# Sigmoid attention and a routed MoE on one core: the splitting block's arm of the run-time loop laid first, the full block's third

## The chip, the cores and the metric

The kernel runs on one core of a Trainium2 chip. The metric is the device time of one execution in microseconds; of several runs the median is given. The profile is of one execution.

## The reference

The first part is attention with a sigmoid in place of the softmax, for 8 batches of 12 heads with 448 tokens of 64 numbers. The second is a mixture of experts over the 3584 resulting tokens of 768 numbers: a token whose skip score is positive goes to the one expert, of eight, with the largest logit.

```python
scores = scale * np.matmul(q, k.transpose(0, 1, 3, 2)) - np.log(S)
attn = 1.0 / (1.0 + np.exp(-scores))
x = np.matmul(attn, v)                      # then as (B * S, H * D)

do_compute = (x @ w_skip) > 0
xc = x[do_compute]
e_idx = np.argmax(xc @ w_gate, axis=1)
for e in range(E):
    h = np.maximum(xc[e_idx == e] @ w1[e], 0.0)
    y[e_idx == e] = gate_w * (h @ w2[e])    # gate_w: softmax weight of the chosen expert
out[do_compute] = xc + y
```

## The kernel before

**Attention.** 48 steps, one for each batch and pair of heads, compute scores (L217), the sigmoid on ACT (L237) and the product with the values (L245). Behind each batch come its logits and its routing: each chosen token's number and gate weight are written to a list in DRAM that has a row range for each expert.

**Experts in straight code.** The expert with the most tokens by an early count is the first one; its weights are loaded and split during attention into a high and a low part (`wh1`, `wl1`, `wh2`, `wl2`). Two blocks of 128 of its tokens are done in straight code behind attention (`b_ph`, `b_py` in the profile). Meanwhile VectorE works out a plan for the rest (L847 to L1050): which block comes in which iteration of a loop, and of which kind it is. The table `slots` gets for each iteration its kind and the next expert to load.

**The loop.** L1493 runs over the remaining blocks. In each iteration every engine reads the kind from `slots` into a register (`entry`, L1054, called in L1494) and branches by itself: first at L1482 on `kind < HALF`, then at L1483 or at L1488. There are four kinds:

- FULL: a block of up to 128 tokens of the expert whose split weights are in place (`block(i, False)`), with three matmuls for each pair of tiles (high by high, low by high, high by low);
- SPLIT: the same, but it is the last full block of its expert, so while it goes on, ACT and VectorE split the next expert's raw weights over the old ones (`block(i, True)`, L1194 to L1203);
- HALF and FEW: up to 64 or up to 32 tokens of an expert that are left over, with unsplit weights (L1414 and L1347). These arms also issue the next expert's weight loads on SP's queue (L1176, L1185).

FULL and SPLIT issue the same matmuls on TensorE: 36 at L496, 48 at L523, 14 transposes, in a slightly different order (`lag` in `gemm1`).

**How the arms lie.** Each engine has an instruction stream of its own. In it the loop is laid out so: the head (hint for the branch at the back edge, reading of the kind, branch of L1482), the branch of L1483, the first arm of the first inner If; then the branch of L1488, and both arms of the second inner If; then the second arm of the first inner If; then the tail, which counts the iteration and branches back at L1493. Before, that is FULL, HALF, SPLIT, FEW. The arms but the last end in a jump to the tail; the profile shows it under the line of the inner If. An arm's first instruction follows the untaken branch where the inner If holds, and is reached by a taken one where it doesn't.

**The order around it.** The order inside an arm is written out by hand (`manual_schedule`, L1477). Between iterations there is no barrier: engines run on by semaphores. `f_last` (L1002) is the kind written for a whole block: a positive value, when the next block is the start of another expert, becomes SPLIT, anything else stays 0, which is FULL. The kinds of the other blocks come from L910 (`HALF - FEW` times a flag, plus `FEW`).

## Time and profile before

| | us |
|---|---|
| median of 3 runs | 535.46 |
| the three runs | 531.62, 535.46, 537.47 |
| the profiled execution | 538.86 |
| its span, from first to last instruction | 537.2 |
| TensorE (PE) busy in it | 506.3 |
| VectorE (DVE), ScalarE (ACT), GpSimd (POOL) busy | 296.9, 274.0, 259.5 |
| mean granted TensorE clock | 0.981 |

A row of the profile names an engine and a line of the kernel. PEld is TensorE's weight load, which runs beside the matmuls (PE). A name with a q (PEldq, ACTq) is the engine's sequencer, that is, the branches, waits and register operations in its queue; those aren't counted as busy. In the chain of waits, each entry is what released the next one; "issue" is time in which the engine waited for nothing that the profile shows. Attention and the straight code take the span up to about 325 us, the loop the rest.

### The profile page before, as it was taken

The numbers are of one execution on the slowest core, as the hardware profiler recorded it, in microseconds if no ns is written. First come the engines' busy times: TensorE is split into PE (matmuls) and PEld (weight loads), VectorE is DVE, ScalarE is ACT, GpSimd is POOL, SyncE is SP. The second block draws the span as 40 slices with busy tenths as digits, with TensorE's granted clock in tenths as the row PEclk, the third lists the DMA queues.
The fourth block names the chain that finished last, engine by engine and source line by source line (L and its number), as shares of the span: only waits on it lengthen the run. The fifth ranks groups of instructions, "written<-read, shape, count | busy, mean of one in ns | idle before, by whom it ended". The sixth has DMA issues, their size and how long they took to land.

```text
span 537.2 us, 15241 instructions
## 1 busy us (share of the span) xinstructions
PE 506.3 (94%) x4985; PEld 337.0 (63%) x4986; DVE 296.9 (55%) x732; ACT 274.0 (51%) x483; POOL 259.5 (48%) x413
## 2 busy tenths in 40 slices
PE   7999999999999999999999998999999999999970
PEld 5555555555555555556446986859587878787850
DVE  4555758568586795675856922962213232369321
ACT  3676766767767566666662122922212323177220
POOL 3523554345566874666674140453324444455642
PEclk8999999999999999999999998999999999999995
DMA  7999897798999899998964046688493959595930
GB/s 207 202 232 221 174 200 152 153 185 176 206 207 233 191 212 197 192 224 168 216 111 95 1 128 245 227 246 299 128 380 108 378 165 381 175 393 163 366 75 7
DMA packets 140481, 107.67 MB, mean 200 GB/s; under 512 B 97013, under 2 KB 112795, under 8 KB 140432
## 3 DMA queue, kind: packets, MB, share of 16 engines
q1 hardware_dynamic: 134096, 97.88, 70.0%
q0 software_dynamic: 4576, 8.66, 7.1%
q8 instruction: 31, 0.51, 0.4%
q10 hardware_dynamic: 1760, 0.48, 0.4%
q14 instruction: 18, 0.15, 0.1%
HBM read 98.93 MB, written 17.60 MB: 217 GB/s over the span
## 4 chain that ended last, share of the span: by engine, by line
PE 74%; DMA 9%; DVE 4%; SPq 4%; issue 3%; ACT 2%; POOL 1%; ACTq 0%; POOLq 0%; DVEq 0%
PE s L217 16%; PE pa L245 14%; PE ph L496 12%; PE py L523 11%; DMA out_dram<-y 4%; PE b_ph L496 3%; PE b_py L523 3%; PE py L1347 3%; PE ph L1347 3%; SPq L268 2%; PE pxt L472 2%; PE py L1414 2%; PE ph L1414 2%; DVE x L202 1%; DMA wr<-in_moe_w_dram 1%
## 5 line engine op out<-in xcount | busy, mean ns | idle before, releaser
L237 ACT ACTIVATE at<-s,bias 128x896 f32<-128x896 f32 x192 | 172.0, 914 | 84.6 <-PE s L217 82.3
L217 PE MATMUL s<-x 64*64 64x448 f32 (+1 forms) x1536 | 166.1, 501 | 7.0 <-DVE x L202 3.3
L245 PE MATMUL pa<-at,v 64*64 64x448 f32 (+1 forms) x1536 | 162.2, 490 | 0.0
L184 POOL COPY kq<-kq 32x896 f32<-32x896 f32 (+1 forms) x96 | 88.2, 919 | 104.6 <-DMA kq<-in_q_dram 62.0
L217 PEld LDWEIGHTS s<-x 64*64 64x64 f32 x1536 | 79.0, 191 | 63.7 <-issue 26.4
L245 PEld LDWEIGHTS pa<-at,v 64*64 64x64 f32 x1536 | 62.0, 133 | 55.7 <-issue 47.6
L202 DVE STREAM_TRANSPOSE x<-kq 128x448 f32<-128x448 f32 x94 | 83.0, 945 | 13.7 <-POOL kq L184 11.8
L255 DVE TENSOR_TENSOR xt<-xt,pa 128x448 f32<-128x448 f32 x48 | 29.5, 614 | 46.1 <-ACT xt L642 42.3
L394 POOL DMA_INDIRECT lst<-rec,idx x32 | 32.3, 1009 | 18.3 <-issue 10.5
L466 POOL TENSOR_TENSOR wl<-wr,wh 128x384 fp32r<-128x384 f32 (+1 forms) x28 | 31.7, 1143 | 8.9 <-DVE wh L465 7.7
L260 DVE STREAM_TRANSPOSE y<-xt 128x448 f32<-128x448 f32 x48 | 31.0, 646 | 4.4 <-DMA out_dram<-y 2.6
L550 POOL DMA_INDIRECT out_dram<-ys,rp x15 | 23.7, 1578 | 15.8 <-issue 8.2
L505 ACT ACTIVATE hs<-ph 128x512 f32<-128x512 f32 x14 | 8.4, 598 | 43.9 <-PE ph L496 35.9
L523 PE MATMUL py<-wh,hh 128*128 128x384 f32 x112 | 29.8, 346 | 0.0
L516 DVE TENSOR_TENSOR hl<-pht,hh 128x512 fp32r<-128x512 f32 x14 | 9.7, 690 | 36.0 <-ACT hh L515 27.6
L523 PE MATMUL py<-wh,hl 128*128 128x384 f32 x112 | 28.8, 338 | 0.0
L523 PE MATMUL py<-wl,hh 128*128 128x384 f32 x112 | 28.7, 337 | 0.0
L496 PE MATMUL ph<-wh,xh 128*128 128x512 f32 x84 | 26.3, 410 | 2.6 <-issue 2.6
L496 PE MATMUL ph<-wl,xh 128*128 128x512 f32 x84 | 27.2, 410 | 0.0
L482 DVE TENSOR_TENSOR xl<-pxt,xh 128x384 fp32r<-128x384 f32 x30 | 15.3, 552 | 20.7 <-PE py L1347 8.9
L642 ACT ACTIVATE xt<-pa 128x448 f32<-128x448 f32 x48 | 25.7, 536 | 1.9 <-PE pa L245 1.3
L496 PE MATMUL ph<-wh,xl 128*128 128x512 f32 x84 | 25.2, 404 | 0.0
(273 smaller groups left out, 666.9 us busy)
## 6 DMA issues: line engine op xcount, KB each, us to landing
raw<-in_moe_w_dram SPq DMA_DIRECT2D x64, 768.0 KB
v<-in_v_dram SPq DMA_DIRECT2D x48, 256.0 KB
out_dram<-y SPq DMA_DIRECT2D x192, 56.0 KB
kq<-in_k_dram SPq DMA_DIRECT2D x46, 224.0 KB
kq<-in_q_dram SPq DMA_DIRECT2D x46, 224.0 KB
wr<-in_moe_w_dram SPq DMA_DIRECT2D x12, 256.0 KB
wr<-in_moe_w_dram SPq DMA_DIRECT2D x16, 192.0 KB
lst<-fill SPq DMA_DIRECT2D x4, 464.0 KB
```

The source lines that it names most:

```text
L184: nc.gpsimd.tensor_copy(a[BT:, :, :, :BT], a[:BT, :, :, BT:])
L202: nc.vector.transpose(xs[:, n].rearrange("p (r j) -> p j r", j=NJ), t.rearrange("p (j d) -> p j d", d=D)[:, :, :BT],)
L217: nc.tensor.matmul(sc[m * D : (m + 1) * D, j, : qs.stop - qs.start], xs[r, 0, first::NR7], xs[r, 1, qs], start=True, stop=True,)
L237: nc.scalar.activation(at[:, :, :n], sc[:, :, :n], AF.Sigmoid, bias=bias, scale=SCALE)
L245: nc.tensor.matmul(pa[j * D : (j + 1) * D, r, qs], vt[rs, j, r + c if c < 3 else 3 * (1 - r), :], at[rs, j, : qs.stop - qs.start], start=( ...
L255: nc.vector.tensor_tensor(x, x, pa[:, 1, :S], op=ALU.add)
L260: nc.vector.transpose(y, xts[b][:, hp, :])
L394: put = nc.gpsimd.indirect_dma_start(out=lst[:, :], out_offset=bass.IndirectOffsetOnAxis(ap=idx[:, c : c + 1], axis=0), in_=rec[:, c, :], ...
L466: nc.gpsimd.tensor_tensor(lo, r, hi, op=ALU.subtract)
L496: nc.tensor.matmul(ph[h], a[:, j * P : (j + 1) * P], w[j][h], start=(n == 0), stop=(n == len(t) - 1),)
L523: last = nc.tensor.matmul(py[:, o, :H2], a[h][:, js], w[j][:, o * H2 : (o + 1) * H2], start=(j == 0 and n == 0), stop=(j == NK2 - 1 and n ...
L1347: nc.tensor.matmul(dst[g * SM : (g + 1) * SM, :n], a, w, start=(j == 0), stop=(j == most - 1), tile_position=(0, g * SM),)
```

## The change

The kinds are renumbered so that SPLIT is 0 and FULL is 3; FEW and HALF keep 1 and 2. The arms of SPLIT and FULL change places in `choose`, so that the streams hold SPLIT, HALF, FULL, FEW. `f_last` is computed with the opposite comparison: a positive value becomes 0 (SPLIT), anything else becomes 3 (FULL). The bound given for the kind, the largest number, is 3 as it was. What the arms compute, and in which order the blocks come, is the same.

```diff
-    FULL, FEW, HALF, SPLIT = range(4)
+    SPLIT, FEW, HALF, FULL = range(4)
...
-    V.tensor_scalar(f_last, f_last, 0.0, float(SPLIT), op0=ALU.is_gt, op1=ALU.mult)
+    V.tensor_scalar(f_last, f_last, 0.0, float(FULL), op0=ALU.is_le, op1=ALU.mult)
...
     arms = {
+        SPLIT: lambda i: block(i, True),
         FULL: lambda i: block(i, False),
-        SPLIT: lambda i: block(i, True),
         HALF: half,
         FEW: few,
     }
...
         with tc.If(kind < HALF) as c:
             with tc.If(kind < FEW) as d:
-                run(FULL, i)
+                run(SPLIT, i)
             with d.Else():
                 run(FEW, i)
         with c.Else():
-            with tc.If(kind < SPLIT) as d:
+            with tc.If(kind < FULL) as d:
                 run(HALF, i)
             with d.Else():
-                run(SPLIT, i)
+                run(FULL, i)
...
-        kind = entry(TYP, ds(i + 2, 1), mybir.ALL_ENGINES, SPLIT)
+        kind = entry(TYP, ds(i + 2, 1), mybir.ALL_ENGINES, FULL)
```

## Prediction

> **What bounds the kernel now.** I read the page first, for the engine that has no slack, then the chain of waits around the start of the loop, then the branches of the lines that the change touches.

> ```profile
> span 537.2 us, 15241 instructions
> PE 506.3 (94%) x4985; PEld 337.0 (63%) x4986; DVE 296.9 (55%) x732; ACT 274.0 (51%) x483; POOL 259.5 (48%) x413
> ...
> q8 instruction: 31, 0.51, 0.4%
> ```

> PE works for 94% of the span. q8 is a queue that carries code: 31 pieces, 0.51 MB, so 16 KB each. The chain from 322 us on (start, length, what):

> ```profile
> 322.07 3.16 PE b_py L523 x18
> 325.23 2.54 issue
> 327.77 8.08 PE ph L496 x27
> ...
> 340.53 7.37 PE py L523 x42
> 347.90 5.30 PE ph L1414 x24
> ...
> 360.13 6.50 PE ph L496 x27
> ...
> 466.62 2.91 PE py L1347 x32
> 469.53 6.50 PE ph L496 x27
> ```

> Almost everything in it is PE. The one hole in the loop is at its entry: 2.54 us in which PE waits for nothing that the profile knows. Inside the loop one iteration follows the other without a gap: 340.53 + 7.37 is 347.90, where the next arm's matmuls (L1414, `half`) begin, and 466.62 + 2.91 is 469.53. So what is saved or lost on PE in the loop moves the end by as much.

> The lines of the choice show what the hole is. First the branch at L1488 at the entry, then at the end of the first iteration, then later; last L1482 over the whole loop (count, min/median/max in ns, first and last start):

> ```profile
> L1488 ACTq COMPARE_BRANCH  x1: 93/93/93, 323.7 to 323.7; - x1
> L1488 PEldq COMPARE_BRANCH  x1: 3435/3435/3435, 324.2 to 324.2; - x1
> L1488 DVEq COMPARE_BRANCH  x1: 122/122/122, 327.3 to 327.3; - x1
> ...
> L1488 PEldq COMPARE_BRANCH  x2: 73/136/198, 344.6 to 346.3; - x2
> ...
> L1488 PEldq COMPARE_BRANCH  x5: 73/193/209, 356.7 to 484.8; - x5
> ...
> L1482 PEldq COMPARE_BRANCH  x14: 74/83/397, 323.7 to 511.8; - x14
> ```

> The first iteration goes past L1482 to L1488 and from there to the arm of kind 3: a splitting block. On PE's queue that jump took 3.435 us; later ones on this line took 0.073 to 0.209 us. On ACT and DVE the same jump took 0.093 and 0.122 us. So it is PE's own code. The code queue, over the stretches 0 to 324, 322 to 326 and 332 to 334 us:

> ```profile
> q8 instruction: 29, 0.48, 0.7%
> ...
> q8 instruction: 1, 0.02, 2.0%
> ...
> q8 instruction: 1, 0.02, 2.9%
> ```

> With PE's counts up to the loop, and in one FULL, one HALF and one FEW arm (us, busy and count of PE, PEld, DVE, ACT, POOL, then PE's clock, DMA share, GB/s):

> ```profile
> 0.00:322.70 322.70, 313.45 (x3714) 185.99 (x3716) 212.74 (x510) 198.79 (x267) 169.44 (x210) 0.99 0.84 178
> ...
> 417.30:435.50 18.20, 18.20 (x98) 16.26 (x97) 4.54 (x14) 5.00 (x14) 6.91 (x20) 1.00 0.86 325
> 348.00:360.10 12.10, 11.98 (x67) 5.25 (x65) 7.64 (x17) 4.87 (x16) 6.61 (x13) 1.00 0.69 192
> 409.50:417.00 7.50, 6.82 (x88) 4.11 (x85) 3.16 (x12) 2.46 (x12) 4.55 (x11) 1.00 0.61 159
> ```

> 3714 + 3716 instructions over 29 pieces is 256 a piece: while PE works through one piece, about one is fetched. A block arm is 195 matmuls and weight loads, HALF 132, FEW 173, and each has some 20 to 35 waits and register operations besides (an estimate from the counts of such rows). I take 215, 165 and 210: the loop is 820 instructions with its head and tail, 3.2 pieces. FULL and HALF together are 380, so the splitting arm begins 1.5 pieces behind the loop's head. That was too far: one piece came at 322 to 326 us while the branch waited, the last one between 332 and 334, and between 340 and 537 us the code queue has no row at all. From there on the whole loop stays where PE can reach it.

> **The change part by part.** The sums are made against the profiled execution: 538.86 us, a span of 537.2 and 1.66 around it. The median shown is 535.46, 3.4 less, and the three runs lie between 531.62 and 537.47; a difference of these sums is carried over to the median as it is.

> *The entry.* The splitting arm is now the first: L1482 and L1483 aren't taken (74 to 83 ns at L1482), and PE runs on into the arm. It is there at 324.0, and the matmuls ahead last until 325.23. The operands are ready too:

> ```profile
> 323.03 1.02 DVE L482 TENSOR_TENSOR xl<-pxt,xh 128x384 fp32r<-128x384 f32 x2 [3.41 <-ACT xf L1062]
> ```

> So the 2.54 us go.

> *The clock behind the hole.*

> ```profile
> 322.50:325.90 3.40, 2.71 (x16) 2.39 (x14) 1.67 (x4) 0.85 (x7) 0.00 (x0) 1.00 0.02 5
> 325.90:329.30 3.40, 1.53 (x7) 1.29 (x8) 0.49 (x1) 0.00 (x0) 1.04 (x1) 1.00 0.78 237
> 329.30:332.70 3.40, 3.40 (x10) 2.62 (x9) 0.00 (x0) 0.00 (x0) 0.00 (x0) 0.50 1.04 371
> ```

> In 325.9 to 329.3 PE was busy for 1.53 of 3.40 us, and for the next 3.4 us it was granted half its clock. The first 27 matmuls took 8.08 us where the same group takes 6.50 at 360.13: 1.58 us, and these go with the hole. Gain so far: 2.54 + 1.58 = 4.12 us.

> *The arm's far end.* Every arm ends in a jump to the loop's tail. Before, the tail lay one FEW arm (210, 0.8 piece) behind the splitting arm; now HALF, FULL and FEW lie between, 590 instructions or 2.3 pieces. [...] I expect the wait of the entry to come again here: 3.435 in place of the 0.198 of the row from 344.6, so 3.24 more. What covers it: that jump starts at 344.6, PE's queued work lasts until 347.90, and the next arm's first wait starts at 346.6:

> ```profile
> L1414 PEldq EVENT_SEMAPHORE  x6: 51/51/51, 346.6 to 347.8; - x6
> ```

> So 1.3 us at most are spare, less some of these waits; I take 1.1, and PE stands idle for 2.1 us (1.9 to 2.4). Half the clock can follow, for 0 to 1.58 us: the busy share ahead of the throttled stretch was 45%, ahead of an unthrottled one 80%, and a hole of 2.1 us leaves between 38% and 70% of a 3.4 us stretch busy, by where it falls. Net: -4.12 + 2.1 + (0 to 1.58) = -2.0 to -0.4. I take the middle, -1.2.

> [...]

> *The FULL arms.*

> ```profile
> L1483 PEldq COMPARE_BRANCH  x15: 73/189/224, 358.3 to 511.9; - x15
> ```

> Of the 14 iterations, the 8 branches at L1488 (one into and one out of an arm) make 4, two of them splitting; the 15 at L1483 (two of a FULL arm, one of a FEW arm, behind which the tail follows at once) make five FULL and five FEW. The FULL arms now pass two taken branches (about 0.2 us each) where they had two untaken ones (0.08), some 0.25 us more each, and the second splitting arm 0.25 less. PE's queue hides that: at 469.53 the old splitting arm, which took both, followed a FEW arm, the shortest cover, without a gap. If it weren't hidden it would be 5 x 0.25 - 0.25 = 1.0 us. On ACT, DVE and POOL the arms trade places in loops whose branches never waited (93 and 122 ns above). SP leaves the first iteration with nothing to issue until 350.78, so a wait of a few us there is covered.

> ```profile
> 350.78 0.39 SPq L1176 DMA_DIRECT2D raw<-in_moe_w_dram  x1
> ```

> *The kinds.* L1002 keeps one instruction with another comparison and constant; the table has the same size. Nothing.

> **The rivals.** *The tail is there in time* (-4.1 us: 531.3). For it: the arm runs for 20 us, and PE keeps more than two pieces. Against it: up to 324 us the pieces came one for one with the work, and 1.5 pieces ahead of it nothing was there.

> *The new fetch stands behind the expert's weights* (slower). The entry's fetch met an idle DMA (share 0.02). The new one falls at 344.6 - 4.1 = 340.5, when the weights still arrive:

> ```profile
> 340.20:343.60 3.40, 3.40 (x23) 3.40 (x21) 3.40 (x7) 3.36 (x8) 2.60 (x5) 1.00 0.63 243
> 343.60:347.00 3.40, 3.40 (x21) 3.40 (x20) 3.05 (x6) 3.40 (x7) 2.52 (x4) 1.00 0.43 120
> ```

> For it: behind the entry's jump (over at 327.6) the next piece came only after 332, 4.4 us on, with the DMA at 0.78 to 1.04. Against it: by 343.6 most of the weights are in. If the fetch waits for that, the stall grows by up to 343.6 - 340.5 = 3.1 us: -4.12 + 2.1 + 3.1 + 1.58 = +2.7, 538.1. With half the clock behind the hole, it is slower than before from 0.4 us of waiting on.

> *It isn't the code's distance*: the first branch of a loop is slow wherever it goes (L1482 too had its 397 ns at the entry). Then the wait stays at the entry and nothing changes, 535.5. Against it: the piece fetched in just that stretch, and the other engines' quick jumps.

> **How the numbers follow.** Wait moved to the arm's end, -2.0 to -0.4: 0.5, 534.3. Gain kept, -4.1: 0.2, 531.3. Behind the weights, up to +2.7: 0.2, 538.1. Nothing: 0.1, 535.5. The range, 530.7 to 538.7, takes in all four with 0.6 us on either side for the spread of the runs. A change of 1% is 5.4 us, about what a measurement of this kernel can tell from none; no case reaches it, and only the spread of runs could carry the second (faster 0.07) or the third (slower 0.05) beyond it; same 0.88.

> **What would show it.** Right: no "issue" row of over 0.3 us at the loop's entry, full clock there, no L1488 or L1483 branch of PE over 0.5 us near 324, but one of 3 us or more at the first arm's end, with an "issue" row of about 2 us ahead of L1414 and a code piece in the same stretch. Wrong: a long branch still at 324; or none anywhere (then 531); or one of over 4 us (then above 535.5). If the entry's hole goes and the end doesn't move although no new hole is seen, PE wasn't the bound there, and my first step fails.

## The result, and the profile after

The changed kernel is a little slower: a median of 537.65 us over 14 runs (534.08 to 541.18) against 533.56 over 14 runs of the kernel before (531.22 to 537.47). The ratio is 1.0069, with a 95% interval from 1.0046 to 1.0092, or +3.7 us (+2.5 to +4.9). Its profiled execution took 536.12 us, 534.4 of them span.

The wait moved as forecast, and it is larger in its new place. PE's branch into the first splitting block, now on L1483, and its jump at that block's end (count, min/median/max in ns, first and last start):

```profile
L1483 PEldq COMPARE_BRANCH  x1: 68/68/68, 321.9 to 321.9; - x1
...
L1483 PEldq COMPARE_BRANCH  x1: 5247/5247/5247, 338.4 to 338.4; - x1
```

The 3435 ns of the entry have become 68; the 198 ns of the jump at the end have become 5247. Two windows from the entry on (us, busy and count of PE, PEld, DVE, ACT, POOL, then PE's clock, DMA share, GB/s) show PE without a gap and at full clock:

```profile
322.90:326.30 3.40, 3.40 (x16) 2.59 (x15) 1.14 (x2) 0.00 (x0) 1.04 (x1) 1.00 0.56 142
326.30:329.70 3.40, 3.40 (x18) 2.71 (x17) 0.00 (x0) 1.05 (x2) 0.00 (x0) 1.00 0.98 330
```

The HALF arm that follows, in order of time on PE (start, length, what, in brackets the idle time before it):

```profile
345.70 8.36 PE L1414 MATMUL ph<-raw,xf 128*64 128x512 f32 x24 [4.02 <-issue]
```

The same 24 matmuls took 5.30 us before. Why they take longer stands in the windows of the clock:

```profile
338.02:341.43 3.41, 3.41 (x21) 3.34 (x19) 3.29 (x6) 3.41 (x7) 2.42 (x4) 1.00 0.99 383
341.43:344.84 3.41, 0.26 (x2) 0.00 (x0) 3.35 (x8) 2.69 (x4) 0.19 (x1) 1.00 0.04 13
344.84:348.26 3.42, 2.56 (x6) 1.14 (x8) 3.26 (x5) 0.00 (x0) 2.23 (x1) 0.50 0.16 10
348.26:351.67 3.41, 3.41 (x10) 1.44 (x8) 0.54 (x2) 0.00 (x0) 0.00 (x0) 0.50 0.66 105
```

PE idles from 341.69 on, and two windows of half the clock follow. So the account at this place is -2.54 (entry) - 1.58 (its half clock) + 4.02 (new hole) + 3.06 (8.36 - 5.30) = +2.96 us. Measured from the end of the last `b_py` group to the end of the HALF arm's `py`, both kernels' chains give it: before 325.23 to 360.13, which is 34.90; after, by the following two rows, 323.18 to 360.99, which is 37.81, 2.91 more.

```profile
320.02 3.16 PE b_py L523 x18
...
355.61 5.38 PE py L1414 x32
```

What the jump waits for is the code queue again. Bytes and packets by queue in the changed kernel, first from 338.4 to 341.2 us, then from 341.2 to 342.4:

```profile
q1 hardware_dynamic: 274, 0.78, 71.4%
q0 software_dynamic: 69, 0.33, 30.4%
...
q0 software_dynamic: 40, 0.07, 15.5%
q8 instruction: 1, 0.02, 5.7%
```

For 2.8 us after the jump only weights (q1) and rows (q0) move; the piece of code comes when they end. The arm's own semaphores aren't what holds it: ahead of its first matmul PE's waits at L1414 last 51 ns each, as before.

```profile
L1414 PEldq EVENT_SEMAPHORE  x10: 51/51/51, 345.4 to 346.9; - x10
```

One thing in these two profiles misleads. The changed kernel's span is shorter (534.4 against 537.2), though by 14 runs each it is the slower one. Cut into stages, the 2.9 us lost at the start of the loop are there, but the FEW arms of the first profile were slower and its attention ended 2.05 us later (325.23 against 323.18) with the same code. The idle time of ACT ahead of L1364, the line in the FEW arm that takes the first product, by what ended it (us, times), first in the kernel before:

```profile
  PE pxt L472: 35.0, 4
  PE ph L1347: 1.0, 1
```

and in the changed kernel:

```profile
  PE ph L1347: 33.3, 5
```

In four of five FEW arms of the one profile ACT went on only after a later group of PE (pxt) than the one it needs (ph). The experiments come back to it.

### The profile page after: what moved, and what is told of

Read it like the earlier page. It is cut to its first block, busy times and chain, and to the rows that moved or that the text cites. A ratio compares the mean times of both kernels' runs of the same rounds, so it can differ in the third digit from the quotient of the medians.

```text
span 534.4 us, 15251 instructions
## 1 busy us (share of the span) xinstructions
PE 506.4 (95%) x4985; PEld 338.7 (63%) x4986; DVE 297.5 (56%) x732; ACT 273.2 (51%) x483; POOL 258.9 (48%) x413
## 4 chain that ended last, share of the span: by engine, by line
PE 71%; DMA 10%; DVE 5%; SPq 4%; issue 4%; POOL 2%; ACT 1%; ACTq 0%; POOLq 0%; DVEq 0%
PE s L217 16%; PE pa L245 14%; PE ph L496 10%; PE py L523 9%; PE b_ph L496 3%; PE b_py L523 3%; DMA raw<-in_moe_w_dram 3%; PE py L1347 3%; PE ph L1347 3%; PE ph L1414 3%; PE py L1414 2%; PE pxt L472 2%; DMA out_dram<-y 2%; DMA kq<-in_q_dram 2%; PE pl L277 1%
## 5 line engine op out<-in xcount | busy, mean ns | idle before, releaser
L523 PE MATMUL py<-wh,hh 128*128 128x384 f32 x112 | 29.8, 347 | 0.0
L523 PE MATMUL py<-wh,hl 128*128 128x384 f32 x112 | 28.8, 338 | 0.0
L482 DVE TENSOR_TENSOR xl<-pxt,xh 128x384 fp32r<-128x384 f32 x30 | 15.3, 551 | 24.2 <-PE py L1414 12.7
L523 PE MATMUL py<-wl,hh 128*128 128x384 f32 x112 | 28.7, 337 | 0.0
L496 PE MATMUL ph<-wl,xh 128*128 128x512 f32 x84 | 26.6, 404 | 0.0
L496 PE MATMUL ph<-wh,xh 128*128 128x512 f32 x84 | 25.7, 403 | 0.0
L1282 DVE TENSOR_SCALAR ys<-py,recs 128x384 f32<-128x384 f32 (+1 forms) x18 | 10.4, 612 | 25.6 <-PE py L523 20.5
```

What stands on the lines that cost most here:

```text
L496: nc.tensor.matmul(ph[h], a[:, j * P : (j + 1) * P], w[j][h], start=(n == 0), stop=(n == len(t) - 1),)
L523: last = nc.tensor.matmul(py[:, o, :H2], a[h][:, js], w[j][:, o * H2 : (o + 1) * H2], start=(j == 0 and n == 0), stop=(j == NK2 - 1 and n ...
```

## Experiments

Theory Q: the jump waits for a piece of PE's code, which is fetched behind transfers that are queued already; it costs PE 3.4 us when the DMA is idle and 5 or more among the expert's weights. Rival D: the jump's price is set by how far it goes (2.3 pieces now, 1.5 before), whatever else is moving. Rival E: the change loses elsewhere, and the hole is chance or of no weight.

**Both kernels again.** No edit; second profiles, on one chip.

> The kernel before, unchanged, for a second profile. Theory (code distance): the hole at the loop's entry is there again, 2.5 us in the chain of waits between b_py and the first ph, with a branch of PE on L1488 of about 3.4 us, and a window of half the clock behind it. Rival (what the first profile showed was chance): no such branch. Open besides: the FEW arms that follow a FULL one took about 0.64 us longer in the first profile of the kernel before than in that of the changed kernel; if the layout makes that, it is here again, if chance, it is gone.

> The changed kernel once more, for a second profile. Theory (the tail's code is fetched behind the expert's weights): at the end of the first splitting block PE's branch on L1483 takes over 4.5 us again (5.2 in the first profile), the hole ahead of L1414 is about 4 us, and its first 24 matmuls take 8.4 us at half the clock instead of 5.3. Rival (chance): the branch takes 3.4 us as the one at the entry did before, with a hole of about 2 us.

The kernel before took 533.2 us, the changed one 537.3. The chain of the kernel before:

```profile
321.41 3.16 PE b_py L523 x18
324.57 2.49 issue
327.06 6.54 PE ph L496 x27
...
352.52 5.38 PE py L1414 x32
```

The hole is there again, but without half the clock behind it: 6.54 us, not 8.08. The changed kernel's jump, and its HALF arm in order of time on PE:

```profile
L1483 PEldq COMPARE_BRANCH  x1: 5142/5142/5142, 340.9 to 340.9; - x1
```
```profile
348.22 7.16 PE L1414 MATMUL ph<-raw,xf 128*64 128x512 f32 x24 [3.98 <-issue]
```

Branch and hole repeat to 0.1 us; the cost of the clock differs (1.86 us here, 3.06 in the first profile). So the hole isn't chance. The FEW arms' slowness is gone from the kernel before (5 of 5 released by ph, 33.3 us), so it doesn't belong to its layout.

**Less and more weights.** In the changed kernel the first load of `w2` is left out, or made twice.

```diff
     for g in range(4):
-        load_w2(g, nx)
+        pool.memset(raw2g[g], 0.0)
```

> The changed kernel without the first load of w2 (its four transfers ahead of the loop; the tiles are set to zero by POOL instead, so the first expert's second matrix is left out of the result). The weights' transfers then end about 7 us earlier, near 335 us. Theory (the fetch stands behind the weights): the jump at the end of the first splitting block, at about 338, meets an idle DMA, takes about 3.4 us as the entry's did before, and the hole ahead of L1414 shrinks from 4.0 to about 2.2 us. Rival (the distance alone, or another cause in PE's queue): the jump still takes 5.2 us and the hole is 4 us.

With half the weights, the jump, and the HALF arm's first group in order of time on PE:

```profile
L1483 PEldq COMPARE_BRANCH  x1: 3559/3559/3559, 338.1 to 338.1; - x1
```
```profile
343.75 7.16 PE L1414 MATMUL ph<-raw,xf 128*64 128x512 f32 x24 [2.34 <-ACT wh L1200]
```

The same jump over the same distance now takes 3.56 us and the hole is 2.34. Q said 3.4 and 2.2; D, with 5.2 and 4, is out. (The releaser named in the brackets is the wait that came last by the profile; the waits themselves last 51 ns each.) Of the half clock 1.86 us remain.

```diff
-    for g in range(4):
-        load_w2(g, nx)
+    for g in range(8):
+        load_w2(g % 4, nx)
```

> The changed kernel with the first load of w2 made twice (the second time to the same tiles with the same data). The weights' transfers then end about 7 us later, near 349 us. Theory (the fetch stands behind the weights): the jump at the end of the first splitting block takes 5.2 + 7 = about 12 us and the hole ahead of L1414 is about 11 us. Rival (the distance alone): the jump still takes 5.2 us and the hole 4; only later arms may wait for weights.

PE in order of time within the first splitting block, and its jump:

```profile
343.55 1.01 PE L523 MATMUL py<-wh,hh 128*128 128x384 f32 x2 [12.41 <-ACT hh L515]
```
```profile
L1483 PEldq COMPARE_BRANCH  x1: 3339/3339/3339, 351.3 to 351.3; - x1
```

Neither theory's number: the jump took 3.34 us. Each second load waits on SP's queue for the first one into the same tile, so SP issued its last load only at 340.4 us; ACT's first split of the new weights stood for SP until 341.3 (14.8 us by the profile), PE in the splitting block stood for ACT (12.4 us; 545.9 us in all), and the jump came at 351.3, when the weights were in. The reading fits Q, but it is no test of it: a dose of traffic that also holds up the arm moves the jump out of the traffic.

**The weights 4 us earlier, in both kernels.** This is the test that takes distance out: one edit, which puts the entry's jump into the weights and the end's jump behind them (where only the next block's rows still move).

```diff
     for j in range(2, NK2 - 3):
-        gemm2(j, hh0, hl0, py)
+        done = gemm2(j, hh0, hl0, py)
...
     for j in range(NK2 - 3, NK2):
-        done = gemm2(j, hh0, hl0, py)
+        gemm2(j, hh0, hl0, py)
```

> The kernel before with the weights' transfers let go one group of matmuls earlier: the second load of w1 waits for the gemm2 group that ends near 320.8 us instead of the last one, so the weights arrive from about 321 to 338 us and the jump at the loop's entry, near 324, falls among them. Theory (a code fetch waits behind the weights that are queued): PE's branch on L1488 takes 5.2 us or more (14 us if the fetch had to wait for all of them), the hole at the entry grows from 2.5 to 4.3 us or more, and half a clock follows: 2 to 5 us more than the kernel before, ratio 1.003 to 1.01. Rival (the jump costs what its distance makes it): 3.4 us, hole 2.5, ratio 1.0.

> The same edit in the changed kernel: the weights arrive from about 321 to 338 us, so they are in, or nearly, when PE jumps to the loop's tail at about 338.4. Theory (the fetch waits behind the weights): this jump takes 3.4 to 3.6 us instead of 5.2, the hole ahead of L1414 is 2.2 to 2.4 us instead of 4.0, and some half clock follows still: about 2 us less than the changed kernel, ratio to the kernel before 1.002 to 1.005. Rival (distance alone): 5.2 us and a hole of 4.0, ratio 1.007. The same edit makes the one kernel's jump longer and the other's shorter only if the weights are what the fetch waits for.

The kernel before with this edit, first the branch, then the chain:

```profile
L1488 PEldq COMPARE_BRANCH  x1: 5840/5840/5840, 319.9 to 319.9; - x1
```
```profile
320.96 4.95 issue
325.92 8.78 PE ph L496 x27
```

The changed kernel with it, the jump and the HALF arm:

```profile
L1483 PEldq COMPARE_BRANCH  x1: 3579/3579/3579, 338.0 to 338.0; - x1
```
```profile
343.69 7.16 PE L1414 MATMUL ph<-raw,xf 128*64 128x512 f32 x24 [2.35 <-ACT wh L1200]
```

The entry's jump grew from 3.4 to 5.84 us, the end's shrank from 5.2 to 3.58, as Q said and D cannot. Against the kernel before the one is at 1.0117 (1.0057 to 1.0177) and the other at 1.0014 (0.9987 to 1.0042). And the fetch doesn't wait for all of the weights. The queues of the first of the two from 319.9 to 323.2 us, and from 323.2 to 324.3:

```profile
q1 hardware_dynamic: 660, 1.29, 104.3%
...
q1 hardware_dynamic: 210, 0.42, 100.5%
q8 instruction: 1, 0.02, 5.5%
```

The code came 3.4 us after the jump, with the weights running on until 334 (a DMA share of 0.93 to 1.06 from 321 to 333 us). Nor does it wait for all that SP had issued by then: that was five loads of 0.79 MB each, of which 1.1 MB had moved, and the code came after 1.3 MB of the 2.8 MB left. What sets its place among the transfers isn't shown.

**The weights earlier still.** In the kernel before the dependency of the second load on `done` is taken out.

```diff
-        if n == 1:
-            tc.add_manual_dep(load.ins, done.ins.name, ...)
```

> The kernel before without the wait that holds the weights' second and later transfers back until the last matmul group ahead of the loop (the dependency on done in the loads of w1). The weights' transfers then begin before PE's jump at the loop's entry. Theory (a code fetch stands behind the weights): PE's branch on L1488 at the entry takes over 5 us instead of 3.4, as many more as the weights need to drain. Rival (the jump costs what its distance makes it): 3.4 us as before. Its whole time also holds the later rows and records, so only the branch is read.

This one decides nothing: the branch took 3.42 us, but the rows of the first block came late behind the weights, the jump moved to 328.74, where its code came after 0.6 us: the weights had just ended (a DMA share of 0.84 in the 0.6 us ahead of the fetch, 0.10 from 329.3 to 330.7 us).

Put side by side, from the traces (us; share: DMA share from the jump until its code comes):

| run | jump at | code comes after | share till then | jump takes |
|---|---|---|---|---|
| before | 324.17 | 0.65 | 0.00 | 3.44 |
| before again | 323.60 | 0.55 | 0.14 | 3.30 |
| more weights | 351.33 | 0.95 | 0.10 | 3.34 |
| less weights | 338.10 | 1.31 | 0.83 | 3.56 |
| changed, weights early | 338.03 | 1.32 | 0.76 | 3.58 |
| changed, hinted, HALF arm's end (below) | 350.88 | 2.28 | 1.05 | 4.54 |
| changed, three profiles | 338.4 to 340.9 | 2.66 to 2.87 | 1.00 to 1.01 | 5.04 to 5.25 |
| before, weights early | 319.91 | 3.36 | 1.06 | 5.84 |

**PE told ahead of the jump.** A hint, the instruction that the loop's head has for its back edge, is put into PE's queue: in the kernel before 80 matmuls ahead of the loop for the branch L1488, in the changed one at the head of the splitting arm for the jump at its end.

```diff
...
+    br = [i for i in pe(branch_block) if "ranch" in type(i).__name__ and "Hint" not in type(i).__name__][-1]
+    loc = nc.tensor.mark_branch_hint_location("LikelyTaken")
+    loc.bb = blocks[at_block]
+    loc.prev_inst_name = pe(at_block)[at].name
+    BassInstruction(br).branch_hint(loc)
```

> The kernel before with one instruction more on PE's queue: 80 matmuls ahead of the loop it is told of the branch L1488 that leads to the splitting arm, so that this arm's code can come before it is needed. Theory (the entry's hole is the missing code of the far arm, and it costs 2.5 us of waiting and 1.6 us of half the clock): PE's branch on L1488 takes under 0.5 us, no hole and no half clock at the entry, and no new wait at the arm's end: 4.1 us less than the kernel before, ratio about 0.992. Rival 1 (the code isn't what the branch waits for, or the instruction fetches nothing): as the kernel before, ratio 1.0. Rival 2 (the tail's code is then missing too): a branch of over 3 us at the arm's end, ratio 1.0 to 1.006.

The kernel before with the hint, its branch at the entry:

```profile
L1488 PEldq COMPARE_BRANCH  x1: 3369/3369/3369, 323.6 to 323.6; - x1
```

The branch took 3.37 us, with the hint at 309.8 us, against 3.44 and 3.30 without it; 0.9993 (0.9966 to 1.0021). Rival 1 of this run holds, and by the runs above in its second form: the code is what the branch waits for, but the hint at that place didn't bring it earlier.

> The changed kernel with one instruction more on PE's queue: at the head of the splitting arm PE is told of the jump that ends this arm, so the loop's tail can be fetched at about 323 us, before the weights' transfers begin (325 to 331 us). Theory (what makes the change slower is the fetch of the tail behind the weights, 4.0 us of hole and 3.1 us of half clock): the jump takes under 0.5 us, the hole ahead of L1414 is gone, 7.1 us less than the changed kernel, ratio to the kernel before about 0.994 to 0.992. Rival (the change loses elsewhere): ratio stays near 1.007.

Branches and chain of this run:

```profile
L1483 PEldq COMPARE_BRANCH  x1: 442/442/442, 338.6 to 338.6; - x1
...
L1488 PEldq COMPARE_BRANCH  x1: 4538/4538/4538, 350.9 to 350.9; - x1
```
```profile
341.94 5.30 PE ph L1414 x24
...
354.29 3.01 issue
357.30 6.54 PE ph L496 x27
```

Here the hint worked for its jump: 0.44 us, no hole ahead of L1414, no half clock. But the wait moved on once more: the next arm, HALF, ends in a jump to the same tail, and that one took 4.54 us, among the next expert's weights (share 1.05), with a hole of 3.01. 1.0054 (1.0025 to 1.0082), so nothing was won. The code queue also has five pieces from 330 us to the loop's end (at 335.1, two at 341.5, at 353.2 and at 483.6) where the changed kernel has two (336.6 and 341.3), so in this run more code was fetched. Why the tail's code was at hand at 338.6 and not at 350.9 isn't shown by these runs.

**Another order of the arms.** FULL, SPLIT, HALF, FEW.

```diff
-    FULL, FEW, HALF, SPLIT = range(4)
+    FULL, SPLIT, HALF, FEW = range(4)
...
         with tc.If(kind < HALF) as c:
-            with tc.If(kind < FEW) as d:
+            with tc.If(kind < SPLIT) as d:
                 run(FULL, i)
             with d.Else():
-                run(FEW, i)
+                run(SPLIT, i)
         with c.Else():
-            with tc.If(kind < SPLIT) as d:
+            with tc.If(kind < FEW) as d:
                 run(HALF, i)
             with d.Else():
-                run(SPLIT, i)
+                run(FEW, i)
```

> Another order of the arms in PE's stream: FULL, SPLIT, HALF, FEW (the kernel before: FULL, HALF, SPLIT, FEW). The splitting arm begins 0.9 pieces of code behind the loop's head (before: 1.5, changed: 0.1) and its end lies 1.5 pieces from the tail (before: 0.8, changed: 2.3). Theory (a jump is slow when its target isn't in PE's own piece or in the one fetched ahead): no hole at the entry; at the arm's end the tail is in the next piece, which is asked for when PE enters the arm's last piece, while the weights arrive, so a stall of 0 to 3 us with a hole of 0 to 2: ratio 0.992 to 1.0. Rival (only the first place in the stream is quick at the entry): the hole of 2.5 us at the entry stays.

The chain, and PE's branches on the three lines over the whole loop:

```profile
319.30 3.15 PE b_py L523 x18
322.44 6.46 PE ph L496 x27
...
340.96 5.30 PE ph L1414 x24
...
347.80 5.38 PE py L1414 x32
```
```profile
L1482 PEldq COMPARE_BRANCH  x21: 83/189/312, 321.0 to 505.0; - x21
...
L1483 PEldq COMPARE_BRANCH  x12: 73/182/380, 321.2 to 503.4; - x12
...
L1488 PEldq COMPARE_BRANCH  x9: 73/218/218, 339.5 to 505.3; - x9
```

No branch of PE takes 0.4 us, `b_py` runs straight into the splitting block and that into the HALF arm, at full clock, and from `b_py` to the HALF arm's end it is 30.73 us (33.33 and 34.90 before, 37.81 after). The ratio is 0.9942 (0.9916 to 0.9968): 3.1 us faster than the kernel before. It beats both kernels. By the estimate of the arms' sizes its exit is 1.5 pieces long, as long as the entry that stalled in the kernel before, so the length alone doesn't tell; the code queue does. Its last piece in the loop comes at 335.2 us and takes 1.1, among the weights, and PE reaches the loop's tail at 338.0: this piece came 2.8 us ahead of the jump. What set its time, and how far ahead PE's code is fetched, these runs don't show.

**The two orders on one chip, and a control.** The order just shown together with the edit that starts the weights 4 us earlier, and beside it the changed kernel, timed again.

> The order FULL, SPLIT, HALF, FEW together with the weights' transfers let go one group of matmuls earlier. A control: in this order no jump of PE near the weights goes to code that is neither at hand nor asked for in time, so the theory (only code fetches behind the weights make the difference between the orders and between the two weight starts) says that the earlier weights change nothing: no hole over 0.5 us between 318 and 360 us, ratio to the kernel before about 0.994 as with this order alone. Rival (the earlier weights themselves cost or bring something): over 0.3% away from that, with PE waiting elsewhere.

> The changed kernel on the same chip as the control, so that the orders SPLIT, HALF, FULL, FEW and FULL, SPLIT, HALF, FEW are timed side by side. Theory: ratio to the kernel before 1.005 to 1.009, a hole of 4 us ahead of L1414 and one or two windows of half the clock behind it. Rival (the first timing was the chip's doing): ratio 1.0. Whether the FEW arms pause in its profile should go with the chip and not with the order, so both kernels of this pair should show the same.

With no jump to miss, the earlier weights change nothing: PE has no hole from 318 to 360 us beyond the half us inside the HALF arm (ACT's ht, L1443) that every chain here has, the stage takes the same 30.74 us, ratio 0.9951 (0.9925 to 0.9976). The changed kernel is at 1.0053 (1.0028 to 1.0079), with its jump of 5.04 us, and in order of time on PE

```profile
347.89 8.07 PE L1414 MATMUL ph<-raw,xf 128*64 128x512 f32 x24 [3.88 <-ACT wh L1200]
```

The FEW arms pause in both of these profiles, and in all four that were taken on the chip of the hints; none of the six taken on the two other chips of these experiments shows it. In these runs it goes with the chip, not with the order. So E is out on both counts: what differs between the layouts is the hole and the clock behind it, and what differed in the rest of the first two profiles isn't theirs.

## Why the prediction was wrong, point by point

Its sign was wrong: -1.2 us was forecast, +3.7 came (+2.9 to +3.4 by the stage in the profiles). The mechanism was right as far as the place and the missing piece of code; three terms of the sum were mis-sized, and the rival that named what sets the price had been given 0.2.

- *The entry* (2.54 us go): right. The branch takes 68 ns and no gap is left.
- *The clock behind the entry's hole* (1.58 us go): only now and then there. Of three profiles of this entry (before, before again, with the hint that did nothing) it shows in one. On average the kernel before had about 0.5 us to lose there, not 1.6.
- *The arm's far end* (3.24 us more on the queue, 1.1 covered, 2.1 of hole, 1.9 to 2.4): this is the step that failed. Place, cause and cover were right: from the jump's start at 338.38, 0.2 us for an ordinary jump and 2.07 from the jump's end to the first matmul would end at 340.65, PE's queue lasts until 341.69, so 1.04 are covered. The jump's price was wrong: 5.25 us, not 3.435, and the 5.05 more than an ordinary jump, less 1.04, is 4.01 (4.02 measured). The price had been taken from a jump that met an idle DMA. With the weights out of the way (less weights; weights early; the next block's rows still moved, at a share of 0.8) nearly the step's own number comes out: 3.56 and 3.58 us, holes of 2.34 and 2.35.
- *Half the clock behind the new hole* (0 to 1.58): 3.06, 1.86 and 2.77 us in three profiles. That the window of the kernel before in which PE was busy for 1.50 of 3.42 us (44%) goes with the half clock of the next was rightly read; but a hole of 4 us leaves one window of 3.41 us at 41% at most wherever it falls (half of it on either side), and in two of the three profiles the first window at half the clock, in which PE started late (2.56 of 3.42 us busy, and 1.96 of 3.41), was followed by another one.
- *The FULL arms' branches and the kinds* (nothing): right. From the HALF arm's end to PE's last matmul it is 158.68 us after and 158.84 before again on chips without the FEW pause, 161.20 after and 161.25 before with it.
- *The rival "behind the weights"* (0.2; up to +2.7): this is what happened, with an account of +2.9. Two things spoke for it in the trace of before, and were weighed too low: the weights' arrival until 343.6 beside the jump at 340.5, and the second piece of code, which came only 4.4 us behind the entry's jump (when that piece was asked for isn't shown). Its reason against, that by 343.6 most of the weights are in, doesn't count: a fetch that comes 2.7 to 2.9 us late has lost them, however few come behind. And the rival's own mechanism was a little off: with 10 us of weights still to come the fetch waited 3.4 us, so it stands behind a part of them, not behind all; how large a part is open.
- *The other two rivals* (0.2 for the tail in time, 0.1 for a slow first branch wherever it goes): out. The jump to the tail took 5.25 us, and the branch at the entry 68 ns.

Sums over the hole and the clock agree with the timing. From `b_py` to the HALF arm's end the three profiles of the entry before take 34.90, 33.33 and 33.35 us, mean 33.86; three of the changed kernel 37.81, 36.60 and 37.46, mean 37.29, so +3.4; the better order 30.73, so -3.1. Timed: +0.69% and +0.53% (3.7 and 2.8 us), and -0.58% and -0.49% (3.1 and 2.6).

The hinted changed kernel is less well accounted for: by its profile, from `b_py` to PE's last matmul, it takes 0.6 us more than the kernel before with the idle hint on the same chip (195.1 against 194.5); timed it is 2.3 us slower (539.28 against 537.01). Its profiled execution, 535.97 us, is near its fastest (535.97 to 541.82) and shows no half clock behind the 3 us hole; whether the slower ones have it stays open.

## What to carry to other kernels

In this run-time loop with its large arms, code was data that had to be moved: PE's jumps to a piece that hadn't come yet took 3.3 to 5.8 us, and in the profile such a jump was a hole (2.5 us of "issue" in the kernel before, 4.0 in the changed one) behind a long branch, with a piece on the code queue. Price such a jump by what the DMA does at that moment, not by another jump; here it was 3.3 to 3.4 us beside a quiet DMA and 4.5 to 5.8 among weights. And lay the arms out for the first iteration: the order that won is the one in which the code of both its entry and its exit had come before the jump, and a change that repairs one end should be checked at the other.

## What the runs showed of the hardware

```profile
341.63:345.04 3.41, 1.35 (x7) 0.90 (x9) 3.19 (x8) 1.73 (x3) 0.78 (x2) 1.00 0.00 0
345.04:348.46 3.42, 3.42 (x11) 1.83 (x9) 2.83 (x5) 0.00 (x0) 1.64 (x1) 0.50 0.39 37
```
```profile
325.66:329.07 3.41, 2.01 (x9) 1.67 (x10) 0.08 (x1) 0.00 (x0) 1.04 (x1) 1.00 0.94 252
329.07:332.49 3.42, 3.42 (x16) 2.74 (x15) 0.00 (x0) 0.86 (x2) 0.00 (x0) 1.00 1.02 375
```

  40% was followed by half the clock, 59% wasn't. So, as an estimate from these windows, a hole of under 1.5 us in otherwise busy work should cost no clock (it leaves at least 55% of any window), and one of over 4.1 us should cost some (a window that holds half of it or more is busy for under 40%); between them the phase plays a part, as the profiles of the same 2.5 us hole show. Neither end was tried. Behind a window that was at half the clock already, more work didn't end it: 2.56 us of 3.42 busy (75%) were followed by another one in the changed kernel.
- The FEW arms' waits on PE ended some 0.6 us later on some chips, and the loop's rest was 2.4 us longer with it in both layouts (161.25 against 158.84 us in the kernel before, 161.20 against 158.68 in the changed one). What it comes from wasn't tried.
